# Ten even/odd sums accumulated in one PSUM bank, and three even halves moved ahead to around the logits

## The chip, the cores and the metric

The kernel runs on one core of a Trainium2 chip. The metric is device time in microseconds (us). Most executions of one kernel on one chip agree within about half a per cent; on the third chip of this study they spread over 1.5. A run is slow when it is over 1.5% above the fastest run of the same kernel. The engines are TensorE (PE in the profile; PEld is its weight load), VectorE (DVE), ScalarE (ACT), GpSimd (POOL) and SyncE (SP).

## The reference

A two-dimensional Fourier transform of each of eight batches, of which the real part is kept, feeds a mixture of experts whose assignment is greedy and global: the largest of all logits first, one expert per token, 2,496 tokens per expert.

```python
X = np.fft.fft(np.fft.fft(x, axis=1), axis=2).real      # x: 8 x 2496 x 256
x = X.reshape(19968, 256)
logits = x @ w_gate                                     # 8 experts
for idx in np.argsort(-logits.flatten()):               # greedy assignment, 2496 tokens an expert
    tok, e = idx // 8, idx % 8
    if assigned[tok] >= 0 or counts[e] >= cap: continue
    assigned[tok] = e; counts[e] += 1
for e in range(8):
    out[assigned == e] = np.maximum(x[assigned == e] @ w1[e], 0) @ w2[e]
```

## The kernel before

It has three stages. In the first (to about 98 us), x is loaded and transformed along its rows, and small matrices for the logits are prepared; the logits end this stage. In the second, **VectorE works out the assignment** (a chain of dependent steps: maxima, lists, a threshold search, ranks) while TensorE does the transform along the columns beside it. In the third, from 169 us to the end, the experts run, and TensorE is busy almost without a hole (341.04 of 356.60 us in the profile).

The column transform is made of 20 calls, `transform(n)`. Each has an even half and an odd half of ten matmuls, each into a PSUM bank of its own. With even half E and odd half O, the rows that are wanted are E + O and E - O.

```python
def transform(n):
    st = stg.tile([P, NB, 4, D], BF, tag="stage", bufs=4)
    ps = []
    def combine():                                       # run later, by flush()
        nc.vector.tensor_tensor(st[:, :, 0, :], ev, ps[1], op=AL.add)
        nc.vector.tensor_tensor(st[:, :, 3, :], ev, ps[1], op=AL.subtract)
        for q in range(2):                               # mirrored columns, sign turned
            nc.scalar.activation(st[:, :, 1 + q, P + 1:D], st[:, :, 3 * q, P + 1:D], ACT.Copy, scale=-1.0)
        # ... copies on GpSimd, store to DRAM ...
        return 1.3                                       # us of VectorE, for the pace
    for r in range(2):                                   # even half, odd half
        fps = ... psm.tile(tag="to"[n % 2], bufs=1) if r else big_ps("fftps")   # big_ps: tag "h", 3 banks
        # ... ten matmuls into fps ...
        ps.append(fps)
        if r == 0:
            ev = stg.tile([P, NB, D], FT, tag="ev", bufs=2)
            nc.scalar.copy(ev, fps)
        cost = flush()                                   # combine the transform before
        if r == 1:
            pending.append(combine)
        yield cost
```

How much of this is put beside the chain is decided when the program is built, by a model of two clocks: the chain's steps advance VectorE's clock by an estimate, and halves (and, at set places, turns of expert weights) are issued while TensorE's clock is behind it.

```python
def unit():                                              # one half, sometimes a weight turn as well
    cost = next(units, None)                             # ... False is returned when none is left
    clock["PE"] += 1.15; clock["D"] += cost; clock["n"] += 1
    if clock["n"] in TURNS: next(pieces); clock["PE"] += 0.45
for c in first_chain():
    # c: VectorE cost of a step; ... at SYNC, where VectorE waits for TensorE, the clocks are levelled
    clock["D"] += c
    while clock["PE"] < clock["D"] - 1.0 and unit(): pass
```

What is not placed there follows behind the chain, ahead of the experts. I call that the **leftover**.

## Time and profile before

| | before |
|---|---|
| time, median of the first 3 runs | 528.65 us (527.63 to 530.01) |
| span of the profiled execution | 526.0 us |
| last gate sums of the load stage start | 83.40 us |
| first matmul that turns the lists (lt) | 117.31 us |
| threshold's matmul (lev_ps), ranks (rps) | 130.71, 133.61 us |
| first expert matmul (hps) | 169.40 us |
| halves and weight turns placed before the ranks | 21 and 7 |

The rows from the last gate sums to the first expert matmul are milestones in TensorE's timeline; the last row counts instructions in the built program. From the first expert matmul to the end are 526.0 - 169.40 = 356.6 us. TensorE is busy for 341.04 us of them, and the work there is untouched by the change, so a milestone that reaches the experts late is taken to reach the end late. The lines of lt and lev_ps are shown in the prediction, those of the gate sums and the experts here (start, duration, engine and line, operation, tiles):

```profile
83.40 1.92 PE L296 MATMUL yps<-zt,g_sb 128*32 128x512 f32 x12
...
169.40 1.15 PE L1258 MATMUL hps<-xs,zball 128*128 128x384 bf16 x6
```

### The profile page before, as it was taken

What the parts mean: (1) busy time and instruction counts of PE and PEld (TensorE: products, weight loads), DVE (VectorE), ACT (ScalarE), POOL (GpSimd) and SP (SyncE); (2) the same over time, 40 slices, a digit from 0 to 9 for tenths busy, and PEclk for the clock granted to TensorE, in tenths of its full rate; (3) what the DMA queues carried; (4) which work ended last, traced back from release to release, by engine and by line L of the source; (5) the groups of instructions that cost most, each with busy time, mean ns of one, the idle gap of its engine ahead of it and who ended that gap; (6) DMA issues with size and microseconds to landing.
All of it is one profiled execution on the core that took longest, in us unless ns stands there. A gap on an engine that the chain in (4) does not pass through costs nothing. (4 is left out here: it accounts for less than half of the span.)

```text
span 526.0 us, 11245 instructions
## 1 busy us (share of the span) xinstructions
PE 463.3 (88%) x4039; PEld 351.1 (67%) x4039; DVE 374.1 (71%) x963; ACT 335.1 (64%) x760; POOL 316.0 (60%) x362
## 2 busy tenths in 40 slices
PE   0667678787799999999999999999999999999991
PEld 0544436675577665767767787777777777777771
DVE  8789997588876989779879777656644555555540
ACT  7879984156377877777867757556545455555540
POOL 7888825253132565535544446777777777777775
PEclk9968999999999999999999999999999999999997
DMA  8999938168479898422232323332222222222222
GB/s 260 319 282 306 315 118 137 26 237 280 115 234 274 203 223 169 129 92 100 99 99 92 109 79 105 124 126 87 79 84 83 77 86 90 76 71 74 73 82 61
DMA packets 35168, 74.62 MB, mean 142 GB/s; under 512 B 6112, under 2 KB 14346, under 8 KB 35104
## 3 DMA queue, kind: packets, MB, share of 16 engines
q0 software_dynamic: 23296, 42.10, 30.7%
q1 hardware_dynamic: 11808, 31.73, 17.8%
q8 instruction: 33, 0.54, 0.4%
q14 instruction: 31, 0.25, 0.2%
HBM read 51.26 MB, written 32.24 MB: 159 GB/s over the span
## 5 line engine op out<-in xcount | busy, mean ns | idle before, releaser
L1011 ACT ACTIVATE hb<-hps 128x384 bf16<-128x384 f32 (+1 forms) x319 | 142.9, 492 | 53.8 <-PE hps L1258 49.1
L1281 PE MATMUL ops<-w2t,hb 128*128 128x256 bf16 (+1 forms) x1344 | 173.6, 273 | 0.0
L1281 PEld LDWEIGHTS <-hb 128*128 128x128 bf16 (+1 forms) x1344 | 132.3, 99 | 31.6
L1285 POOL DMA_INDIRECT out_dram<-zball,rid x85 | 91.1, 1072 | 77.5 <-ACT zball L1011 59.8
L1258 PE MATMUL hps<-xs,zball 128*128 128x384 bf16 x640 | 127.5, 326 | 0.3 <-ACT hb L1011 0.2
L1258 PEld LDWEIGHTS <-zball 128*128 128x128 bf16 x896 | 84.6, 98 | 45.4 <-issue 7.4
L1015 DVE TENSOR_SCALAR hb<-hps 128x384 bf16<-128x384 f32 (+1 forms) x129 | 70.2, 549 | 45.1 <-PE hps L1258 35.3
L130 POOL DMA_INDIRECT xb<-in_x_dram,mir_i x40 | 54.6, 1364 | 11.9 <-issue 10.5
L1011 ACT ACTIVATE zball<-ops 128x256 f32<-128x256 f32 x82 | 31.5, 384 | 32.1 <-PE ops L1281 31.2
L1258 PE MATMUL hps<-xt,zball 128*128 128x384 bf16 (+1 forms) x256 | 47.7, 319 | 0.0
L286 PE MATMUL tp<-identf,xa 128*128 128x128 f32 x160 | 26.6, 330 | 17.8 <-ACT hi_cE L259 7.5
L286 PEld LDWEIGHTS tp<-identf,xa 128*128 128x128 f32 x160 | 22.8, 172 | 25.4 <-ACT zt L288 7.9
L1042 POOL COPY stage<-stage 128x258 bf16<-128x258 bf16 x40 | 17.6, 444 | 32.0 <-DVE stage L1037 28.5
L1011 ACT ACTIVATE xs<-sps 128x384 bf16<-128x384 f32 x68 | 30.2, 490 | 9.6 <-PE sps L1120 9.5
L1097 DVE TENSOR_SCALAR pt<-rampw,spot 128x193 bf16<-128x193 bf16 (+1 forms) x160 | 30.8, 285 | 0.1
L1120 PE MATMUL sps<-pt,xl 128*128 128x192 bf16 (+1 forms) x320 | 29.4, 232 | 0.1
L1120 PEld LDWEIGHTS <-xl 128*128 128x128 bf16 x320 | 25.6, 98 | 3.6 <-issue 1.4
L1234 POOL DMA_INDIRECT xg<-t_dram,ids_l x24 | 23.1, 963 | 7.3 <-issue 7.0
L1285 POOL DMA_INDIRECT out_dram<-zball,rows_l x23 | 22.3, 970 | 7.0 <-issue 2.7
L1017 DVE COPY zball<-ops 128x256 f32<-128x256 f32 (+1 forms) x26 | 11.0, 424 | 20.4 <-PE ops L1281 17.9
L1060 ACT COPY ev<-fftps 128x512 f32<-128x512 f32 x20 | 11.7, 584 | 21.2 <-PE fftps L1054 12.1
L1285 POOL DMA_INDIRECT out_dram<-wa,rid x20 | 19.8, 989 | 6.1 <-issue 2.7
(358 smaller groups left out, 780.2 us busy)
## 6 DMA issues: line engine op xcount, KB each, us to landing
t_dram<-stage SPq DMA_DIRECT2D x20, 512.0 KB
xl<-t_dram SPq DMA_DIRECT2D x20, 512.0 KB
xa<-in_x_dram SPq DMA_DIRECT2D x8, 1024.0 KB
w1raw<-in_moe_w_dram POOLq DMA_DIRECT2D x8, 512.0 KB, 8.6
w2t<-in_moe_w_dram POOLq DMA_DIRECT2D x8, 512.0 KB, 9.1
xa<-in_x_dram SPq DMA_DIRECT2D x8, 224.0 KB
out_dram<-zball,rid POOLq DMA_INDIRECT x85, 2.5
xb<-in_x_dram,mir_i POOLq DMA_INDIRECT x40, 7.8
```

What stands on the lines that cost most here:

```text
L130: nc.gpsimd.indirect_dma_start(out=bv[0:n, i, :], out_offset=None, in_=x_pairs, in_offset=bass.IndirectOffsetOnAxis(ap=mir_i[0:n, b * NK + ...
L286: nc.tensor.transpose(tp[:, blk, u, :], pv[:, 4 * c + u, blk * P:(blk + 1) * P], identf)
L1011: nc.scalar.activation(dst, src, ACT.Relu if relu else ACT.Copy)
L1015: nc.vector.tensor_scalar(dst, in0=src, scalar1=0.0, scalar2=None, op0=AL.max)
L1042: nc.gpsimd.tensor_copy(st[:, :, 1 + q, 0:P + 1], st[:, :, 3 * q, 0:P + 1])
L1060: nc.scalar.copy(ev, fps)
L1097: nc.vector.tensor_scalar(marks[n][:, f, 0:w], in0=rampw[:, 0:w], scalar1=spot[:, c:c + 1], scalar2=None, op0=AL.is_equal)
L1120: nc.tensor.matmul(into[:, :, SW - SC[cc]:], lhsT=xl[:, 2 * g + cc, j2 * P:(j2 + 1) * P], rhs=pt[:, 2 * g + cc, 0:E * SC[cc]].rearrange("p ...
L1234: nc.gpsimd.indirect_dma_start(out=xg[0:nr, q, :], out_offset=None, in_=t_dram, in_offset=bass.IndirectOffsetOnAxis(ap=d["ids"](q, nr), ax ...
L1258: nc.tensor.matmul(hps[:, 0:n], lhsT=w1t[d["e"]][:, j2, fc * P:(fc + 1) * P], rhs=d["x"](j2), start=(j2 == 0), stop=(j2 == 1))
L1281: nc.tensor.matmul(ops[0:nr, 0:D], lhsT=d["hid"][:, fc, b0:b0 + nr], rhs=w2t[d["e"]][:, fc, :], start=(fc == 0), stop=(fc == F // P - 1))
L1285: put = nc.gpsimd.indirect_dma_start(out=out, out_offset=bass.IndirectOffsetOnAxis(ap=d["rows"](b0 // P)[0:nr], axis=0), in_=ot[0:nr, :], ...
```

## The change

The intent was to relieve VectorE, the fullest engine beside the chain (busy for 31.54 of the 36.42 us from 99.05 to 135.47 us), in two ways. First, in ten of the transforms the odd half is accumulated onto the even half in the same bank, so the bank holds E + O: ScalarE copies that sum out, and VectorE needs only the one difference 2E - (E + O). Second, three even halves run before VectorE's chain begins, one after the gate sums, one after the tables are placed, one after the logits. For that the three "h" banks are taken from a pool that leaves early.

```diff
+SUMS = 10
+DONE = 3
...
     low_y()
     gate_x(B - 1, zts.pop(B - 1))
+    even_ahead(0)
     place_y(B - 1)()
+    even_ahead(1)
...                                   # behind the logits' matmuls
+        even_ahead(2)
...
+    def even_half(n):
+        # ... bank of even_ahead, or a new one of the three; ten matmuls if n >= DONE ...
+        evs[n] = stg.tile([P, NB, D], FT, tag="ev", bufs=3, name="ev")
+        if n < SUMS:
+            nc.scalar.activation(evs[n], fps, ACT.Copy, bias=0.0, scale=2.0)
+        else:
+            nc.scalar.copy(evs[n], fps)
+    def odd_half(n):
+        # ... n < SUMS: ten matmuls that accumulate into the even half's bank ...
         def combine():
-            nc.vector.tensor_tensor(st[:, :, 0, :], ev, ps[1], op=AL.add)
-            nc.vector.tensor_tensor(st[:, :, 3, :], ev, ps[1], op=AL.subtract)
+            if n < SUMS:
+                nc.scalar.copy(st[:, :, 0, :], fps)
+            else:
+                nc.vector.tensor_tensor(st[:, :, 0, :], ev, fps, op=AL.add)
+            nc.vector.tensor_tensor(st[:, :, 3, :], ev, fps, op=AL.subtract)
...
-            return 1.3
+            return 0.7 if n < SUMS else 1.3
+    def halves():
+        for n in range(SUMS + 1):
+            if n < SUMS:
+                even_half(n)
+                if n >= DONE:
+                    yield flush()
+            if n > 0:
+                cost = flush()
+                pending.append(odd_half(n - 1))
+                yield cost
+        # ... then as before ...
-    clock = {"PE": 0.0, "D": 0.0, "n": 0}
+    clock = {"PE": 0.0, "D": 0.0, "n": DONE}
```

While the "h" banks hold sums, weight turns and sorts use the odd halves' banks instead. One of two sort buffers goes.

More of the change, by code (lines that the diff above doesn't have):

```diff
@@ L101 @@
     psl = ps_cm.__enter__()
+    pst_cm = tc.tile_pool(name="psturn", bufs=1, side="right", space=PS)
+    pst = pst_cm.__enter__()
     ab = {}
@@ L281, in turn_x @@
     def turn_x(b, pv, c):
-        tp = psl.tile([P, 2, 4, P], FT, tag="tp", bufs=2, name="tp")
+        tp = pst.tile([P, 2, 4, P], FT, tag="tp", bufs=2, name="tp")
         nn = 4 if c < 2 else 2
@@ L373 @@
             xa_cm.__exit__(None, None, None)
+            pst_cm.__exit__(None, None, None)
         if b > 0:
@@ L385, with half_products, even_ahead @@
             tab_phases()
+    psm = ctx.enter_context(tc.tile_pool(name="psmid", bufs=1, side="right", space=PS))
+    NB = 2
+    begun = {}
+    def half_products(fps, n, r, acc):
+        b0, ks = NB * (n // NK), slice(n % NK * P, (n % NK + 1) * P)
+        for d0, d1, tab in ((0, P + 1, hi["c" + "EO"[r]]), (P + 1, D, hi["s" + "EO"[r]])):
+            for i in range(NK):
+                nv = rows_of(i, r)
+                first = i == 0 and (not acc or (r == 0 and d0 == 0))
+                nc.tensor.matmul(fps[:, :, d0:d1], lhsT=tab[:nv, i, ks],
+                                 rhs=zball[:nv, b0:b0 + NB, 2 * i + r, d0:d1],
+                                 start=first, stop=(i == NK - 1 and (not acc or d0 > 0)),
+                                 skip_group_check=acc)
+    def even_ahead(n):
+        fps = psm.tile([P, 512], FT, tag="h", bufs=3, name="fftps").rearrange("p (b d) -> p b d", b=NB)
+        half_products(fps, n, 0, True)
+        begun[n] = fps
     low_y()
     gate_x(B - 1, zts.pop(B - 1))
+    even_ahead(0)
     place_y(B - 1)()
+    even_ahead(1)
     iota160 = const.tile([P, E * CB], BF, name="iota160")
@@ L482, with mid @@
     moe = ctx.enter_context(tc.tile_pool(name="moe", bufs=1, side="left"))
-    psm = ctx.enter_context(tc.tile_pool(name="psmid", bufs=1, space=PS))
+    pso = ctx.enter_context(tc.tile_pool(name="pso", bufs=1, space=PS))
+    def mid(tag):
+        return pso if tag == "o" else psm
     psr_cm = [tc.tile_pool(name="psasg", bufs=1, space=PS)]
@@ L496, in spread_ps @@
             return deep["ps"].tile(shape, dt, tag=tag + "x", bufs=1, name=nm)
-        return psm.tile(shape, dt, tag=tag, bufs=n, name=nm)
+        return mid(tag).tile(shape, dt, tag=tag, bufs=n, name=nm)
     def big_ps(nm):
@@ L843, in first_strips @@
         flush()
-        bps = psm.tile([P, 512], FT, tag="o", bufs=1, name="lev_ps")
+        bps = mid("o").tile([P, 512], FT, tag="o", bufs=1, name="lev_ps")
         nc.tensor.transpose(bps[:, 0:P], lev.to_broadcast([P, P]), identf)
@@ L856, in first_strips @@
         for e0, ne, tag in ((0, 3, "t"), (3, 3, "o"), (6, 2, "t")):
-            rps = psm.tile([P, 512], FT, tag=tag, bufs=1, name="rps")[:, 0:ne * GC]
+            rps = mid(tag).tile([P, 512], FT, tag=tag, bufs=1, name="rps")[:, 0:ne * GC]
             rv, ov = (v_.rearrange("p (f k) -> p f k", k=NK) for v_ in
@@ L1020 @@
     td_v = t_dram.rearrange("(n p f) d -> n p f d", p=P, f=8)
-    NB = 2
     def flush():
@@ L1027, in flush @@
         return cost
-    def transform(n):
-        b0, kc = NB * (n // NK), n % NK
-        ks = slice(kc * P, (kc + 1) * P)
+    evs = {}
+    def even_half(n):
+        begun[n] = begun.get(n) or big_ps("fftps").rearrange("p (b d) -> p b d", b=NB)
+        fps = begun[n]
+        if n >= DONE:
+            half_products(fps, n, 0, n < SUMS)
+        evs[n] = stg.tile([P, NB, D], FT, tag="ev", bufs=3, name="ev")
[4 more added lines that the diff above has]
+    def odd_half(n):
+        fps, ev = begun.pop(n), evs.pop(n)
+        if n >= SUMS:
+            fps = mid("to"[n % 2]).tile([P, 512], FT, tag="to"[n % 2], bufs=1, name="fftps").rearrange(
+                "p (b d) -> p b d", b=NB)
+        half_products(fps, n, 1, n < SUMS)
         st = stg.tile([P, NB, 4, D], BF, tag="stage", bufs=4, name="stage")
-        ps = []
         def combine():
-            nc.vector.tensor_tensor(st[:, :, 0, :], ev, ps[1], op=AL.add)
-            nc.vector.tensor_tensor(st[:, :, 3, :], ev, ps[1], op=AL.subtract)
+            if n < SUMS:
[3 more added lines that the diff above has]
+            nc.vector.tensor_tensor(st[:, :, 3, :], ev, fps, op=AL.subtract)
             for q in range(2):
@@ L1045, in combine, with side_ps @@
                 reload(n)
-            return 1.3
-        for r in range(2):
-            fps = (psm.tile([P, 512], FT, tag="to"[n % 2], bufs=1, name="fftps") if r else big_ps("fftps")).rearrange(
-                "p (b d) -> p b d", b=NB)
-            for d0, d1, tab in ((0, P + 1, hi["c" + "EO"[r]]), (P + 1, D, hi["s" + "EO"[r]])):
-                for i in range(NK):
-                    nv = rows_of(i, r)
-                    nc.tensor.matmul(fps[:, :, d0:d1], lhsT=tab[:nv, i, ks],
-                                     rhs=zball[:nv, b0:b0 + NB, 2 * i + r, d0:d1],
-                                     start=(i == 0), stop=(i == NK - 1))
-            ps.append(fps)
-            if r == 0:
-                ev = stg.tile([P, NB, D], FT, tag="ev", bufs=2, name="ev")
-                nc.scalar.copy(ev, fps)
-            cost = flush()
-            if r == 1:
-                pending.append(combine)
-            yield cost
+            return 0.7 if n < SUMS else 1.3
+        return combine
+    def halves():
+        for n in range(SUMS + 1):
+            if n < SUMS:
+                even_half(n)
+                if n >= DONE:
+                    yield flush()
[3 more added lines that the diff above has]
+                yield cost
+        flush()
+        side["on"] = False
+        for n in range(SUMS, 4 * NT):
+            even_half(n)
+            yield flush()
+            pending.append(odd_half(n))
+            yield 0.0
+    side = {"on": True, "n": 0}
+    def side_ps(nm):
+        if not side["on"]:
+            return big_ps(nm)
+        side["n"] = 1 - side["n"]
+        return mid("to"[side["n"]]).tile([P, 512], FT, tag="to"[side["n"]], bufs=1, name=nm)
     def turn_w(e, eng=None):
@@ L1074, in turn_pieces @@
             for fh in range(2):
-                wps = big_ps("wps")
+                wps = side_ps("wps")
                 fs = slice(fh * 512, (fh + 1) * 512)
@@ L1099, in sort_mark @@
         busy["D"] += 1.1
-    a8 = [moe.tile([P, 4, 320], BF, name="a8_%d" % i) for i in range(2)]
-    for i in range(2):
-        nc.gpsimd.memset(a8[i], 0.0)
+    a8 = moe.tile([P, 4, 320], BF, name="a8")
+    nc.gpsimd.memset(a8, 0.0)
     def reload(n):
@@ L1115, in sort_call @@
         for g in gs:
-            sps = big_ps("sps")
+            sps = side_ps("sps")
             for cc in range(2):
@@ L1125, in sort_rows @@
     def sort_rows(t, part):
-        a_t = a8[t % 2]
+        a_t = a8
         if part == 1:
@@ L1159 @@
     pieces = (None for e in range(4) for _ in turn_pieces(e, "A"))
-    units = (cost for n in range(4 * NT) for cost in transform(n))
-    clock = {"PE": 0.0, "D": 0.0, "n": 0}
+    units = halves()
+    clock = {"PE": 0.0, "D": 0.0, "n": DONE}
     def unit():
```

## The prediction

> **What bounds the kernel now.** I read the page first, then the windows of the middle stage, then TensorE's waits, then the timelines of the three engines there.
>
> ```profile
> span 526.0 us, 11245 instructions
> PE 463.3 (88%) x4039; PEld 351.1 (67%) x4039; DVE 374.1 (71%) x963; ACT 335.1 (64%) x760; POOL 316.0 (60%) x362
> ...
> PE   0667678787799999999999999999999999999991
> ```
>
> Slices are 13.15 us. From slice 12 (158 us) TensorE shows a 9 to the end, and the window from 300 to 400 us has it busy for 100.00 us: the expert stage is TensorE's, so a start of that stage that moves by x moves the end by about x. Before it TensorE has gaps. The change acts between 85 and 170 us, so I cut that stretch where the assignment chain on VectorE lets go.
>
> ```profile
> core 0: us, PE busy (x) PEld busy (x) DVE busy (x) ACT busy (x) POOL busy (x), PEclk, DMA share, GB/s
> 99.05:135.47 36.42, 30.23 (x254) 24.18 (x255) 31.54 (x73) 17.47 (x38) 15.15 (x37) 1.00 0.60 203
> 135.47:169.40 33.93, 31.13 (x306) 25.40 (x304) 26.36 (x83) 22.41 (x53) 9.45 (x22) 1.00 0.72 205
> ```
>
> In the first window VectorE is the fullest (31.54 of 36.42 us), in the second TensorE (31.13 of 33.93). So the first is a chain on VectorE with transform halves put beside it, the second the transform work that was left over. The waits of TensorE from 99 to 175 us, and where they fall:
>
> ```profile
> PE fftps L1054 <- DVE stage L1038: 3.1, 3, 1.6
> PE lev_ps L845 <- DVE stage L1038: 3.1, 1, 3.1
> PE fftps L1054 <- DVE pool L470: 1.1, 1, 1.1
> PE rps L860 <- DVE ohb L850: 1.1, 1, 1.1
> ```
> ```profile
> 85.88 0.65 PE L306 MATMUL ytp<-identf,yt 96*128 96x96 f32 x4 [0.57 <-ACT yt L299]
> 87.27 0.19 PE L457 MATMUL lps_cE<-yhl,hi_cE 128*128 128x64 bf16 x1 [0.74 <-DVE yhl L310]
> ...
> 99.09 0.72 PE L1054 MATMUL fftps<-zball,hi_cE 128*128 128x258 bf16 x5 [1.14 <-DVE pool L470]
> ...
> 106.36 0.73 PE L1054 MATMUL fftps<-zball,hi_cO 128*128 128x258 bf16 x5 [1.56 <-DVE stage L1038]
> ...
> 117.31 1.04 PE L632 MATMUL lt<-identf,lists_x 128*128 128x128 f32 x8
> ...
> 130.71 0.29 PE L845 MATMUL lev_ps<-identf,s_lev 128*128 128x128 f32 x1 [3.07 <-DVE stage L1038]
> ```
> ```profile
> 101.40 0.59 ACT L1060 COPY ev<-fftps 128x512 f32<-128x512 f32 x1 [9.10 <-DVE lg L474]
> ...
> 105.75 0.41 ACT L1040 ACTIVATE stage<-stage 128x254 bf16<-128x254 bf16 x1 [2.54 <-DVE stage L1037]
> ```
> ```profile
> 103.62 1.49 DVE L599 TENSOR_TENSOR dd<-lg,mx 128x1280 bf16<-128x1280 f32 x1
> 105.03 0.68 DVE L1037 TENSOR_TENSOR stage<-ev,fftps 128x512 bf16<-128x512 f32 x1
> 105.63 0.68 DVE L1038 TENSOR_TENSOR stage<-ev,fftps 128x512 bf16<-128x512 f32 x1
> ```
>
> The reader is to see four things. TensorE's holes before the logits are 0.57 and 0.74 us. ScalarE cannot copy the first even half until 101.40, because the copy's buffer lies where the logits' scratch was (released by the last lg). VectorE's first combination stands behind dd, at 105.03. All of TensorE's waits from 99 to 170 us sum to 9.9 us.
>
> [...] In the kernel before no bank has two readers: ScalarE reads the even bank, VectorE the odd one. In the changed one ScalarE (twice) and VectorE read one bank, and the built program shows the guard: each difference on VectorE waits for ScalarE's copy of the same sum. No run yet shows its price. [...] on ScalarE each even copy starts after the negations queued before it. [...] here ten matmuls of a half take 1.11 us start to start (99.09, 99.64, 100.19)[...].
>
> **The change part by part.** Call the halves of transform n e(n) and o(n).
>
> Saved: ten of 40 VectorE combinations go. Each occupies 0.60 us start to start (105.03 to 105.63), so 6.0 us of VectorE; eight of the differences that stay lie ahead of the strips, where there were 11 pairs, so 14 x 0.60 = 8.4 us go from the chain's own engine. Three halves, 3 x 1.11 = 3.3 us, leave TensorE's stretch after 99 us.
>
> Added: e(0) and e(1) before the logits are 2.2 us into holes of 0.57 and 0.74. e(0) begins at 85.25, ends 86.36, so the transposes move from 85.88 to 86.36; e(1) follows 0.53 us later and ends at 88.00, where the logits began at 87.27: **0.73 us late**. e(2) after the logits takes the place of the 1.14 us wait. Ten copies of 0.59 us come to ScalarE.
>
> Moved, and this decides it. o(n) now accumulates into the bank that e(n) filled, so it waits for the even copy of n. That copy is still bound to the last lg, 101.29 + 0.73: copy 102.13 to 102.72, o(0) at 102.77. e(2) ended at 99.65, so TensorE stands 3.1 us. At 105 us it has done five halves, as before. Then a ring closes. There are three banks, so e(n+3) waits for difference n. ScalarE's order in the built program is even copy n+3, sum copy n+1, negations. Difference n+1 waits for sum copy n+1. From one difference to the next: difference 0.68, semaphore 0.05, e(n+3) until ScalarE starts 1.36 (99.09 to a start 0.09 us after the modeled end), even copy 0.49, sum copy 0.59, 0.04: **3.2 us a transform**, where TensorE needs 2.22.
>
> Walking that: difference 0 stands behind dd at 105.76, differences 1 to 4 come at 108.97, 112.18, 115.39 and 118.60. The chain's lists end behind difference 4, so lt comes at 119.66 instead of 117.31. From there fewer combinations win the time back: search 1 ends 3.4 us late, then TensorE is no longer ahead with two halves and a weight turn, and lev_ps comes at about 130.45 against 130.71. So the chain ends where it did, strips' marks at 141.1.
>
> But by then TensorE has done less. In the order of the two programs 21 halves and seven weight turns stand before the strips' sums (rps) in the kernel before, 18 halves (with the three ahead) and four turns in the changed one. What is left is more by 3 x 1.11 + 3 x 0.43 = **4.6 us**, in the window where TensorE is the bound. Its first half after rps no longer waits (0.58 us saved). Differences 8 and 9 stand behind the marks at 141.1, and with the banks held by them a weight turn waits about 2.2 us and the next steps 1.1 us: 3.3 us against 1.34 at the same place before, 2.0 us more. Sum: 4.6 - 0.6 + 2.0 - 0.1 (chain) = about **5.8 us later** at the experts. By idle time: 9.9 grows to about 18, +8.2, less 3.3 moved, plus 0.7 of delay: 5.6. The two agree.
>
> **Rivals.** First, the ring does not bind (the guard is cheap, the copies prompt). Then lt comes 1.4 us earlier, the strips 5.6 us earlier, and with TensorE's gaps mostly closed the experts start 2 to 5 us sooner: 524 to 527. For it: VectorE is 87% full in the first window and loses 8.4 us. Against: the order and waits of the built program are fixed. Second, hidden anyway: the halves ahead only trade a wait at 99 for one at 102, and the rest evens out: 528 to 530. For it: five halves done at 105 us both ways. Third, worse than walked: ScalarE, with ten more copies, stays behind into the second window and every even copy lags; ScalarE is only 22 of 34 us busy there, so against; 537 to 541. A transfer as the bound I exclude: reloads come tens of us before use, DMA share is 0.6 to 0.7.
>
> **Range and chances.** 528.65 + 5.6 is **534.2 us**. My walk sums some thirty handovers each good to 0.05 to 0.1 us, and the second window's stall to perhaps 2 us, so 529.5 to 538.5 holds it 8 times in 10, the low side leaving room for the second rival. Two per cent are 10.6 us: faster than 518.1 needs twice all that could be won, 0.01; slower than 539.2 needs the third rival, 0.05; within, 0.94.
>
> **What will show it.** Logits start near 88.0. o(0) waits about 3 us for the even copy. VectorE stands about 2.6 us between differences 0 and 1, waiting for ScalarE's sum copy, and differences are 3.2 us apart until lt at about 119.7. TensorE waits for differences at e(4), e(5), e(6), about 1.0 us each. lev_ps near 130.5. The first expert matmul near 175 instead of 169.40. I am wrong if VectorE takes difference 1 at once, if lt comes before 117.3, or if the experts begin before 170; and if they begin at 175 but the end does not move, the expert stage was not TensorE's alone.

The forecast: its sum stays at about 5.8 us (4.6 - 0.6 + 2.0 - 0.1, which as printed make 5.9). The durations in it are those of the profile of before: a half takes 1.11 us start to start (99.09 to 100.19), a weight turn 0.43 (119.30 to 119.73), an even copy 0.49 (119.55 to 120.04), and the 0.05 us called semaphore lie between the end of the 0.68 us at 105.63 and the odd half at 106.36. The 0.59 us of the sum copy and the 0.04 us after it are estimates; the even copy's 0.59 us and the step from the end of the 0.68 us at 105.03 to the negation at 105.75 agree with them. The order on ScalarE reads there, for one, as negations at 105.75 and 106.34, even copy at 106.67. That each difference waits for ScalarE's copy of the sum was read from the built program, and what this costs was not measured then; the profile of after has 8.3 us in six waits. Of the reloads, three are issued from 111.38 to 116.66 us and the first matmul that reads one starts at 149.75; none of the waits of TensorE listed from 99 to 175 us ends with a transfer.

## The result, and the profile after

The changed kernel took 536.41 us (median of 4 runs, 536.15 to 536.95), the kernel before 528.28 us beside it (median of 4). The ratio is **1.015**, interval 1.0123 to 1.0177. Here and below a ratio is the mean time of one kernel's fast runs over that of the other's of the same rounds, so it is not quite the ratio of the medians. The result is correct in all runs told of here.

The page of the changed kernel, in the same rows as before, with the granted clock's row (tenths of full speed; the kernel before has its own in the second fence):

```profile
span 534.3 us, 11214 instructions
PE 468.1 (88%) x4028; PEld 352.5 (66%) x4039; DVE 367.2 (69%) x953; ACT 340.2 (64%) x770; POOL 313.9 (59%) x361
...
PEclk9978889999799999999999999999999999999996
```
```profile
PEclk9968999999999999999999999999999999999997
```

VectorE has ten instructions and 6.9 us less, ScalarE ten more and 5.1 us more: the trade that was intended took place. In the fifth, sixth and eleventh slices the changed kernel's clock shows 8, 8 and 7 where the kernel before has 9; the eleventh is 134 to 147 us, in the stretch that the change acts on, the other two are in the load stage.

TensorE's timeline after, for the places that the prediction walked (start, duration, engine and line, operation, tiles, count, and in brackets the wait before it):

```profile
85.35 1.92 PE L300 MATMUL yps<-zt,g_sb 128*32 128x512 f32 x12
...
104.50 0.72 PE L401 MATMUL fftps<-zball,hi_cO 128*128 128x258 bf16 x5 [2.95 <-ACT ev L1068]
108.22 0.72 PE L401 MATMUL fftps<-zball,hi_cE 128*128 128x258 bf16 x5 [1.33 <-DVE stage L1085]
111.37 0.72 PE L401 MATMUL fftps<-zball,hi_cE 128*128 128x258 bf16 x5 [0.77 <-DVE stage L1085]
...
121.17 1.09 PE L662 MATMUL lt<-identf,lists_x 128*128 128x128 f32 x8 [0.55 <-DVE lists_x L654]
...
132.00 0.29 PE L875 MATMUL lev_ps<-identf,s_lev 128*128 128x128 f32 x1 [1.36 <-DVE s_lev L870]
...
137.50 1.29 PE L401 MATMUL fftps<-zball,hi_cO 128*128 128x258 bf16 x5
...
177.17 1.15 PE L1312 MATMUL hps<-xs,zball 128*128 128x384 bf16 x6
```

VectorE's differences in the same stretch, and what VectorE waited for from 95 to 145 us (total, times, longest):

```profile
107.48 0.68 DVE L1085 TENSOR_TENSOR stage<-ev,fftps 128x512 bf16<-128x512 f32 x1
...
110.63 0.69 DVE L1085 TENSOR_TENSOR stage<-ev,fftps 128x512 bf16<-128x512 f32 x1 [2.47 <-ACT stage L1082]
...
113.78 0.69 DVE L1085 TENSOR_TENSOR stage<-ev,fftps 128x512 bf16<-128x512 f32 x1 [1.06 <-ACT stage L1082]
```
```profile
DVE stage L1085 <- ACT stage L1082: 8.3, 6, 2.5
```

And ScalarE between the first two differences:

```profile
109.52 0.60 ACT L1068 ACTIVATE ev<-fftps 128x512 f32<-128x512 f32 x1 [0.91 <-PE fftps L401]
110.02 0.58 ACT L1082 CAST stage<-fftps 128x512 bf16<-128x512 f32 x1
```

The ring of the prediction can be read off these lines step by step. Difference 0 starts at 107.48 and frees a bank; TensorE takes the next even half (e(3)) at 108.22, after 1.33 us of standing; ScalarE copies it at 109.52, having itself waited 0.91 us for TensorE; only then, at 110.02, does it copy the sum of transform 1, whose matmuls end by 106.9 us but which stands behind the even copy in its queue; and VectorE, which has stood for 2.47 us, starts difference 1 at 110.63. From there to 113.78 are 3.15 us, and the next two differences follow at the same distance. In the kernel before VectorE has no wait of this kind: from 95 to 145 us none of its waits listed ends with ScalarE.

The milestones need one correction before they are compared. The last gate sums start at 83.40 us in the profile of before, at 85.35 in that of after. Over all profiles, whose load stages run the same instructions, this start lies anywhere from 83.39 to 86.75 us. It goes with the clock of that stage: the six profiles with 6.8 to 17.1 us at half clock before 84 us have it at 83.4 to 84.0 us, the eight with 20.5 or 23.9 us at 84.1 to 86.8 us (before 17.1 us, after 20.5 us). So the lateness of 1.95 us belongs to the execution as far as this record shows, and I give milestones **from the start of the last gate sums**:

| from the last gate sums, us | before | after | after, second profile |
|---|---|---|---|
| lt | 33.91 | 35.82 | 36.03 |
| lev_ps | 47.31 | 46.65 | 46.86 |
| rps | 50.21 | 49.61 | 50.75 |
| first expert matmul | 86.00 | 91.82 | 93.25 |
| halves, turns before rps | 21, 7 | 18, 4 | 18, 4 |

The end of the chain stays where it was and the experts are 5.8 and 7.3 us late. From the first expert matmul to the end are 534.3 - 177.17 = 357.1 us, against 356.6. So the loss is made before the experts, and it passes to the end whole.

The windows that the prediction showed of the kernel before, in the profile of after (columns as there):

```profile
99.05:135.47 36.42, 24.77 (x238) 19.30 (x236) 24.48 (x62) 18.36 (x38) 12.48 (x32) 0.97 0.43 160
135.47:175.00 39.53, 37.10 (x300) 29.00 (x304) 27.56 (x83) 25.24 (x59) 10.22 (x23) 0.94 0.72 212
```

VectorE is no longer the full engine beside the chain (24.48 of 36.42 us, was 31.54): it was relieved. But TensorE too did less there (24.77, was 30.23), and made it up in the second window, where it is the bound. The clock is 0.97 and 0.94 in these windows, 1.00 and 1.00 in the kernel before. This was not in the prediction. Its place is clear in a short window, 135 to 141 us, first of before, then of after:

```profile
135.00:141.00 6.00, 5.41 (x45) 4.29 (x44) 5.71 (x23) 1.18 (x2) 0.72 (x1) 1.00 0.22 34
```
```profile
135.00:141.00 6.00, 5.92 (x26) 3.88 (x28) 4.35 (x12) 0.45 (x1) 0.25 (x1) 0.57 0.55 92
```

TensorE is busy for longer (5.92 us against 5.41) with 26 instructions instead of 45: it runs at a granted clock of 0.57. Five matmuls that take 0.72 us elsewhere take 1.29 us there (the line at 137.50 above). The stretch at half clock itself is 133.4 to 140.2 us. Just ahead of it, from 128.7 to 132.1 us, TensorE had stood but for two lone matmuls of 0.16 and 0.29 us (the second is the lev_ps line above), waiting for VectorE's search each time.

So there were two theories to test, and a third that could make either unimportant. **Ring**: the order on ScalarE, even copy before sum copy, is what costs. **Clock**: stop-and-go on TensorE costs, by way of half-clock stretches. **Leftover**: too little TensorE work is placed beside the chain, because the pace now counts 0.7 us a combination.

### The profile page after: what moved, and what is told of

Read it like the earlier page. It is cut to its first block, busy times and chain, and to the rows that moved or that the text cites. A ratio compares the mean times of both kernels' runs of the same rounds, so it can differ in the third digit from the quotient of the medians.

```text
span 534.3 us, 11214 instructions
## 1 busy us (share of the span) xinstructions
PE 468.1 (88%) x4028; PEld 352.5 (66%) x4039; DVE 367.2 (69%) x953; ACT 340.2 (64%) x770; POOL 313.9 (59%) x361
## 5 line engine op out<-in xcount | busy, mean ns | idle before, releaser
L134 POOL DMA_INDIRECT xb<-in_x_dram,mir_i x40 | 54.0, 1349 | 11.9 <-issue 10.2
L349 DVE TENSOR_TENSOR xa<-xa,xb 128x2550 f32<-128x2550 f32 (+2 forms) x10 | 22.8, 2282 | 0.0
```

The lines of the kernel that those rows point to most:

```text
L134: nc.gpsimd.indirect_dma_start(out=bv[0:n, i, :], out_offset=None, in_=x_pairs, in_offset=bass.IndirectOffsetOnAxis(ap=mir_i[0:n, b * NK + ...
L349: nc.vector.tensor_tensor(a_t[:, i0:i1, :, 1:D], a_t[:, i0:i1, :, 1:D], b_t[:, i0:i1, ::-1, D - 1:0:-1], op=AL.add)
```

## The experiments

Twelve runs in three groups; each group shares its runs of the kernel before. The first group's kernel before took 528.96 us, the second's 528.58 us (7 runs each, on two chips). The third group fell on a chip on which the kernel before took 589.27 us; it is told of on its own.

### First group: the ring

**The changed kernel again**, without an edit.

> The changed kernel once more, unedited, for a second profile and as the base of this call. All theories: 536 to 537 us. What it tells apart: in the first profile the logits stage began 1.95 us later than before (first gate sums for the last batch at 85.35 instead of 83.40), and the granted clock was 0.57 from 135 to 141 us. If both are chance of one execution they are gone or smaller here at the same time (534 would be the time without them); if they belong to the kernel they recur.

Measured: 537.32 us, ratio 1.0166 (1.013 to 1.0201). The difference is real and repeats, and so does the ring (3.15 us a difference). This profile has half-clock stretches at 104.0 to 107.4, 131.3 to 134.7 and 144.9 to 148.3 us, of which the first profile had only one like the second, twice as long. The first of them follows the wait of 2.94 us for the even copy. So the half clock recurs, at other places, and the late load stage is smaller (84.14 us).

**Sum copy ahead of the even copy.** `flush()` runs the combination that is pending; moved ahead of the even half, it puts the sum copy and the negations before the next even copy in ScalarE's queue. Nothing else changes, and the counts of halves and turns stay 18 and 4.

```diff
+                cost = flush() if n >= DONE else 0.0
                 even_half(n)
                 if n >= DONE:
-                    yield flush()
+                    yield cost
```

> The sum copy and the negations of an earlier transform are put on ScalarE ahead of the even copy of a later one; TensorE's and VectorE's order stays. Theory A (the ring of difference, even half, even copy, sum copy, difference paces the chain at 3.15 us a transform): the ring has no even half in it any more, VectorE's wait between the first two differences falls from 2.5 to about 1.1 us, lt comes 2 to 3 us earlier, and the time falls to 532 to 534. Theory B (too little TensorE work was put beside the chain, so what is left over decides; the ring is slack): lt earlier or not, the time stays at 535.5 to 536.5.

Measured: 531.18 us, ratio **1.0038** (1.0005 to 1.0071). The first five differences now follow at 1.6 to 2.5 us, and VectorE's wait for sum copies falls from 8.3 to 3.8 us, shown in the second fence over the same 95 to 145 us:

```profile
107.56 0.68 DVE L1085 TENSOR_TENSOR stage<-ev,fftps 128x512 bf16<-128x512 f32 x1
109.19 0.69 DVE L1085 TENSOR_TENSOR stage<-ev,fftps 128x512 bf16<-128x512 f32 x1 [0.95 <-ACT stage L1082]
...
111.71 0.69 DVE L1085 TENSOR_TENSOR stage<-ev,fftps 128x512 bf16<-128x512 f32 x1 [0.44 <-ACT stage L1082]
```
```profile
DVE stage L1085 <- ACT stage L1082: 3.8, 5, 1.4
```

From the last gate sums, lt comes at 32.96, lev_ps at 42.26, the experts at 87.73. The ring was there, and moving two lines recovers about 6 of the 8 us. But one thing does not fit if the ring is all: the chain now reaches lev_ps 5.1 us sooner than in the kernel before, and yet the experts start 1.7 us later. Between lev_ps and the experts 45.47 us pass, against 38.69 in the kernel before: 6.8 us more, with the same 18 halves and 4 turns placed before the ranks as in the changed kernel. That speaks for the leftover as a second part.

**Difference ahead of the sum copy.** Here VectorE's read of the bank is put first, and ScalarE's copy behind it.

```diff
         def combine():
-            if n < SUMS:
-                nc.scalar.copy(st[:, :, 0, :], fps)
-            else:
+            if n >= SUMS:
                 nc.vector.tensor_tensor(st[:, :, 0, :], ev, fps, op=AL.add)
             nc.vector.tensor_tensor(st[:, :, 3, :], ev, fps, op=AL.subtract)
+            if n < SUMS:
+                nc.scalar.copy(st[:, :, 0, :], fps)
```

> In the combination the difference on VectorE goes ahead of the sum copy on ScalarE, so ScalarE waits for VectorE in the shared bank and not the reverse; same instructions. Theory A: VectorE no longer waits for ScalarE's sum copies (8.3 us of waits fall below 2), differences follow TensorE at about 2.2 us, lt comes about 3 us earlier, the strips 4 us earlier, 531 to 534. Theory B: the chain ends earlier, but TensorE's leftover does not shrink and ScalarE's later copies hold banks: 535 to 537.

Measured: 532.54 us (531.34 to 536.54), ratio 1.0061 (1.0031 to 1.009). VectorE has no wait for a sum copy left, and differences 0 and 1 run back to back. What comes instead is on TensorE: it waits for ScalarE's copies, now the last to read a bank, 2.8 us once and 1.1 us once, and in the profiled execution, which was the slowest of the five, its clock is half from 106.6 to 113.5 us, and the third difference stands 2.98 us for TensorE. So lt comes at 37.56 us from the last gate sums, later than in the changed kernel: the "3 us earlier" missed in this execution, while the times held.

**Sum copied by VectorE.** One word is changed, `nc.scalar.copy` to `nc.vector.tensor_copy`. The bank then has one reader, and VectorE gets its ten instructions back.

> The sum copy goes to VectorE as well, so no two engines share a bank's readers apart from the even copy; VectorE gets back the ten operations that the change took from it. Theory A: no wait of VectorE on ScalarE's sum copies, lt near the kernel before plus 0.7 to 1.5 us, 531 to 535. Theory B (VectorE's saved work is what counts, and its loss hurts): slower than the changed kernel, above 537.

Measured: 533.42 us (531.17 to 535.28), ratio 1.0075 (1.0027 to 1.0122). Here too differences 0 and 1 follow at once, and here too the third comes late, in a half-clock stretch (105.5 to 112.3 us). lt comes at 34.78, 0.9 us later than in the kernel before, as expected.

What follows from the four: each of three different ways to open the ring wins 4 to 6 us of the medians against 537.32. Which way matters less than that it is open. None reaches the kernel before.

### Second group: the clock, and the two parts of the change alone

**Waits filled.** Matmuls whose results nobody reads are put where TensorE stands: the third even half is computed three times and the eleventh twice, and 15 wide matmuls go into the banks of the second search's sum, of lev_ps and of rps. The outcome is the same numbers.

```diff
+        for _ in range(2):
+            half_products(begun[2], 2, 0, True)
...
+    def fill(ps, k):
+        for _ in range(k):
+            nc.tensor.matmul(ps, lhsT=onesb, rhs=..., start=True, stop=True)
...
+        fill(bps, 5)                       # lev_ps; 7 in the search, 3 in rps
...
+            for _ in range(1+1 if n == SUMS else 1):
                 half_products(fps, n, 0, n < SUMS)
```

> The changed kernel with idle matmuls (results never used, or the same half computed again) in TensorE's waits before o(0), the second search sum, lev, rps and after e(10): 15 of 512 columns and three halves again, sized to end before the wait does. Theory C (beside the ring, the stop-and-go of TensorE lets its granted clock fall to 0.50 for 3.4 us or multiples of it between 100 and 150 us, which none of it did in the kernel before): the dips at 104 to 112, 130 to 140 and 144 to 148 us are gone or fewer, the time falls from 537 by 1.5 to 3 us to 534 to 535.5 although TensorE has 6.5 us more to do. Rival (the dips fall into time that TensorE waits anyway): the time stays at 536 to 538.

Measured: 534.35 us (533.92 to 535.62), ratio 1.0113 (1.0081 to 1.0144). From 84 us to the experts its profile has no stretch under full clock, the ring is unchanged (3.15 us), and the window around the dip in the changed kernel reads as follows, first of the changed kernel, then of the filled one:

```profile
132.00:141.00 9.00, 8.12 (x39) 5.11 (x41) 7.15 (x17) 2.06 (x4) 1.20 (x2) 0.62 0.51 118
```
```profile
132.00:141.00 9.00, 7.95 (x58) 5.59 (x57) 7.73 (x23) 2.57 (x5) 1.24 (x2) 1.00 0.55 117
```

So useless work made the kernel 2.1 to 3.0 us faster (against 536.41 and 537.32). The intervals of the ratios overlap at their ends, and the 537.32 us are from another chip, so the size is rough; the clock column is not. Nor does all of it lie in the stretch that was filled: from the gate sums, the experts start at 91.51 us, only 0.3 and 1.7 us sooner than in the two profiles of the changed kernel.

**Waits filled in the kernel with the sum copy ahead.** The same fillers, in slightly other numbers, on top of copy_first.

> The version with the sum copies ahead of the later even copies (531.2), with idle matmuls in the same waits (15 of 512 columns and four halves again). Theory C: no dips of the clock from 100 to 150, and with the ring and the dips both gone the three halves that were moved show at last: 526.5 to 529. Rival: 530.5 to 532.

Measured: 529.96 us, ratio 1.0026 (0.9989 to 1.0064), between the two expectations; no clock dip from 84 us to the experts, which start 86.83 us from the last gate sums. Against copy_first that is 1.2 us by the medians, inside the intervals, so whether the filling won anything here is not shown. This is the fastest of the changed kernels on the two fast chips, and not told apart from the kernel before.

**Halves ahead only.** SUMS is 0, so all twenty transforms have two banks and two VectorE operations, and the three even halves still go ahead.

```diff
-SUMS = 10
+SUMS = 0
...
-            yield flush()
+            if n >= DONE:
+                yield flush()
```

> Only the three even halves ahead; each transform keeps two banks and two operations on VectorE (no sums). Theory A (ring from the sums in one bank is the main cost): no ring, no wait of o(0) for the even copy; TensorE has 3.3 us less to do after the logits, which start 0.73 us later, while all three big banks are taken at 99 us: 526 to 529.5. Rival (the halves ahead are themselves the loss, through the later logits and the banks they hold): 531 to 534.

Measured: 536.43 us, ratio 1.0146 (1.0117 to 1.0174). **Both expectations missed.** The profile tells of two things. The three banks stay held until combination 0, which stands behind VectorE's own steps, so TensorE waits 6.6 us in one piece at 109 us. And the pace, which counts three halves as done and a full 1.3 us a combination, puts 18 halves and 4 turns ahead of lt, where the changed kernel has 13 and none: lt comes at 46.51 us from the last gate sums, not 35.82. So this run does not measure one part alone. It shows only that the halves ahead did not pay in this form.

**Sums only.** DONE is 0 and the three `even_ahead` calls are gone.

> Only the sums in one bank for the first ten transforms; no half ahead of or right behind the logits. Theory A: the ring is there as in the changed kernel (differences 3.15 us apart, VectorE waits 7 to 9 us for sum copies), and 3.3 us of TensorE work return to the stretch after 99 us: 536 to 540. Rival (the sums are harmless or good without the halves ahead): 526 to 531.

Measured: 533.12 us, ratio 1.0088 (1.0053 to 1.0123), between the two expectations. The ring is there (gaps of 0.77 us on TensorE again), a clock dip between 84 us and the experts is not, and lt and lev_ps come sooner than in the kernel before (30.44 and 42.18 against 33.91 and 47.31), because the pace places only 9 halves ahead of lt. The experts come at 89.70, 3.7 us late: only 16 halves and 2 turns stand before the ranks. Again a chain that is early and experts that are late.

### Third group: the pace, on a slower chip

On this chip the kernel before took 589.27 us (583.3 to 592.31, 11 runs, two of them slow; 588.81 without these). In the four profiles taken here the extra 60 us are in the expert stage. From 300 to 400 us TensorE is busy for 100.00 us in copy_first on the fast chip, and for 87.82 us in copy_first_mid here; what makes the holes was not looked into. From the first expert matmul to the end the four profiles have 417.5, 414.6, 416.1 and 417.3 us. That stage alone scatters by 3 us, which is what the experiments are about, so the times decide little, and **I read the milestones instead, which lie before the experts**. There is one profile of each, and none of the kernel before on this chip.

**Sum copy ahead, and a pace of 1.0 us**, in place of 0.7: more work beside the chain.

```diff
-            return 0.7 if n < SUMS else 1.3
+            return 1.0 if n < SUMS else 1.3
```

> copy_first with one number changed: the pace counts 1.0 us instead of 0.7 us of VectorE for a combination whose sum ScalarE copies, so that more TensorE work is put beside the chain. In the built order 20 halves and 6 weight turns stand before the strips' sums, where copy_first has 18 and 4 and the kernel before 21 and 7. Theory L (the leftover is what keeps copy_first from beating the kernel before): 2 halves and 2 turns, 3.1 us, move from the stretch in which TensorE is the bound into gaps beside the chain, of which TensorE had about 5 us in copy_first, so the experts begin 1 to 3 us sooner and the time is 528 to 530.3. Rival (the work merely delays the chain by as much as it takes off later): 530.5 to 532, lev_ps about 3 us later than in copy_first.

Measured: 588.08 us (587.32 without one run of the slow state), ratio 0.9999 (0.9931 to 1.0066). TensorE's first expert matmul, first of copy_first (its last gate sums start at 85.16), then of this kernel (85.54):

```profile
172.89 1.15 PE L1313 MATMUL hps<-xs,zball 128*128 128x384 bf16 x6
```
```profile
169.48 1.15 PE L1313 MATMUL hps<-xs,zball 128*128 128x384 bf16 x6
```

The experts start at 83.94 us from the last gate sums: 3.8 us sooner than in copy_first and 2.1 us sooner than in the kernel before. lev_ps is 2.8 us later than in copy_first, as the rival had it, and the experts come sooner all the same. The clock is a rival for a part of the 3.8 us: this profile has 3.4 us at half clock between 84 us and the experts, that of copy_first 6.8 us.

**Sum copy ahead, and the old pace of 1.3 us.** The edit is `return 1.3`.

> As copy_first_mid, with the old 1.3 us: 24 halves and 8 turns before the strips' sums. Theory L: TensorE has no gap left beside the chain but the chain's own matmuls now stand behind more work, so the gain stops: 528 to 531, lev_ps 3 to 5 us later than copy_first. Rival (the leftover is the whole rest of the cost, so more is better): 526 to 528. Second rival (the chain becomes the bound): over 532.

Measured: 588.93 us, ratio 1.0039 (0.997 to 1.0109). The experts start at 85.38, so 2.4 us sooner than in copy_first but 1.4 later than with 1.0. lev_ps is 8.2 us later than in copy_first, more than the 3 to 5 expected. Of the three paces tried, 1.0 us has the earliest experts, as the leftover theory had it; here the profile has 6.8 us at half clock again.

**Sums only, sum copy ahead.** The edit of copy_first on sums_only.

> sums_only with the even copy behind the sum copy on ScalarE: no halves ahead, ten sums in one bank, no ring. Pace as in sums_only, so 16 halves and 2 turns before the strips' sums. Theory A (the ring is the main cost wherever sums are shared): differences under 2.7 us apart, lt 1 to 2 us sooner than sums_only's 114.0, and the time 1.5 to 4 us under sums_only: 529.5 to 531.5. Rival L (in sums_only the leftover is the cost, not the ring, since TensorE is the bound behind the strips and the chain has slack): no VectorE wait on sum copies, lt and lev_ps sooner, but the experts begin no sooner: 532 to 534.

Measured: 594.48 us, ratio 1.0141 (1.0075 to 1.0208), which the verdict calls unclear and which is not better than the 1.0088 of sums_only on the other chip. By milestones lt comes 1.6 us sooner than in sums_only (28.82) and the experts 2.4 us sooner (87.29), as theory A had it; the first differences are 2.1, 2.1 and 3.2 us apart, so "under 2.7" holds for most of them. Neither of the two profiles has a half-clock stretch between 84 us and the experts, so the clock is no rival here. The time does not show this, and I leave it open.

**Even copies with a place of their own.** The buffers of the even copies move to a pool that does not lie on the logits' scratch, so the first three need not wait for the last lg.

```diff
+    evp = ctx.enter_context(tc.tile_pool(name="evp", bufs=1, side="left"))
...
-        evs[n] = stg.tile([P, NB, D], FT, tag="ev", bufs=3, name="ev")
+        evs[n] = evp.tile([P, NB, D], FT, tag="ev", bufs=3, name="ev")
```

> The changed kernel with the buffers of the even copies in a place of their own, so that the first three need not wait for the last lg. My walk put 3.1 us of TensorE's standing at the first odd half down to this wait, but holds the first difference to stand behind dd all the same, with all banks taken until it runs: the wait moves from the first odd half to the fourth even half, lt stays within 0.7 us of the changed kernel's 120.2, and the time is 535.5 to 537.5. Rival (the wait at the first odd half is itself a part of the loss): lt 2 us sooner, 533 to 535.

Measured: 598.51 us, ratio 1.0205 (1.0143 to 1.0266). The wait at the first odd half is gone, and the fourth even half waits 4.5 us for the first difference in its place, the longest of five here:

```profile
PE fftps L401 <- DVE stage L1086: 6.8, 5, 4.5
```

From the second on, differences stay 3.15 us apart, and lt comes at 36.96, about 1 us later than in the two profiles of the changed kernel (the expectation allowed 0.7), not 2 us sooner. The first difference starts where it did, 22.2 us from the last gate sums against 22.1, and the second comes 4.2 us behind it, in a half-clock stretch (107.8 to 111.2 us). The rival falls: the wait of 2.95 us that stands out first in TensorE's list was only a place where TensorE stood, not a cause.

The milestones together, all from the last gate sums in us:

| kernel | lt | lev_ps | experts | halves, turns before rps | us at half clock, 84 us to the experts |
|---|---|---|---|---|---|
| before | 33.91 | 47.31 | 86.00 | 21, 7 | none |
| after | 35.82 | 46.65 | 91.82 | 18, 4 | 6.8 |
| copy_first | 32.96 | 42.26 | 87.73 | 18, 4 | 6.8 |
| copy_first_mid | 35.35 | 45.09 | 83.94 | 20, 6 | 3.4 |
| copy_first_full | 38.80 | 50.43 | 85.38 | 24, 8 | 6.8 |
| sums_only | 30.44 | 42.18 | 89.70 | 16, 2 | none |

## Why the prediction was right or wrong

It said 534.2 us and within 2 per cent; the time was 536.41 us, inside its range, 1.5 per cent slower. By its own steps:

- **Logits late by 0.73 us**: from the last gate sums the first logits matmul is 4.62 us (89.97 us in the profile) against 3.87, 0.75 later. Held.
- **First odd half waits 3.1 us for the even copy**: 2.95 and 2.94 us in two profiles. Held as a wait. copies_early shows that it is not a loss of its own, which the walk implied, since it had difference 0 behind dd either way.
- **Ring of 3.2 us**: 3.15 us, and the stall before difference 1 was 2.47 us against 2.6. Held, down to the order of the queue. copy_first opens it and wins about 6 us. In milestones the ring had eaten the 4.4 us by which lev_ps then comes sooner (42.26 against 46.65).
- **TensorE's waits at e(4) to e(6), "about 1.0 us each"**: 0.77 us each, the first at e(3) 1.33. Slightly over.
- **lt at 119.66, lev_ps at about 130.45, experts near 175**: 119.22, 130.05 and 175.22 when the profile is shifted to the load stage of the kernel before (less 1.95 us). Held.
- **Leftover of 4.6 us more, and 2.0 us of a stall, less 0.6**: 6.0 us more between lev_ps and the experts than in the kernel before. Measured 6.5 and 7.7 us in the two profiles of the changed kernel, which have half-clock stretches there, and 6.0 in the filled one, which has none (but one half more). Its parts held less well than their sum: the weight turn that was to wait about 2.2 us waited 1.04 and 2.37 us. copy_first_mid points to such work being worth about what was counted: 2 halves and 2 turns (3.1 us) put back beside the chain went with experts 3.8 us sooner. One profile each, on two chips, with 3.4 us less at half clock.
- **The sum, about 5.8 us** (the terms as printed make 5.9, and the 534.2 us takes the 5.6 of the count by idle time): the medians differ by 8.1 us, and the time is 2.2 us over the 534.2. The mechanism was right, the sum short. **What it left out is TensorE's clock**: it counted every half at 1.11 us, at full clock. Between 84 us and the experts the two profiles of the changed kernel have 6.8 and 10.2 us at half clock, that of the kernel before has none. With the waits filled, no dip and the ring untouched, the time is 534.35 us, 5.8 us over the kernel before of its chip. How much of the 2.2 us the change makes is not settled: against the filled kernel, the two profiles lose 0.3 and 1.7 us between the gate sums and the experts, and 1.6 and 0.4 us in the load stage, where the three run the same instructions.
- **Luck in one profile.** In the first one the experts are 5.8 us late from the gate sums, as walked, although 6.8 us there ran at half clock. Two errors met: the slow matmuls, and the weight turn's wait of 1.04 us where 2.2 was forecast. In the second profile that wait is 2.37 us and the experts are 7.3 us late.
- **A miscount without consequence**: ahead of the marks at 141.1 us the trace of the kernel before has ten pairs of combinations, not 11 (the eleventh starts at 141.13), so 12 x 0.60 = 7.2 us go from VectorE there, not 8.4. Only the first rival used the number.

Of its rivals, the first (no ring) falls by the 3.15 us, the second (hidden anyway) by the interval, and the third (ScalarE behind) was not needed: ScalarE has 25.24 of 39.53 us in the second window.

Of the missed term the runs show this: the granted clock in the dips is 0.50; between 84 us and the experts they last 3.4 or 6.8 us; their places differ between executions of one kernel (133.4 us in the first profile of the changed kernel, 104.0, 131.3 and 144.9 us in the second); and in the two filled kernels there are none. In the changed kernel 3.4 us with two lone matmuls of 0.16 and 0.29 us were followed, 1.3 us later, by half clock. One wait of 2.95 us was not followed by it, those of 2.94 and 3.0 us in the next profile and in vec_copy were. What brings the half clock, and how little activity is enough for it, these runs do not show. I had read waits as idle time only, and did not ask what they do to the clock, although the page of the kernel before shows a clock of 0.6 in its third slice, in the load stage.

Open: whether the change also shifts the load stage a little on the average (its end scatters by 3.4 us, and there is one profile of before), what slows the experts on the third chip, and the time of copy_first_mid on a fast chip, where its milestones suggest some 2 us under the kernel before.

## What to carry to other kernels

Where two engines read one PSUM bank, one waited for the other here (VectorE for ScalarE's copies 8.3 us in six waits, and 3.8 us in five when the copies came first in ScalarE's queue), so ask what else stands ahead in each engine's queue: an order of two copies on ScalarE was worth 6 us, nearly as much as the 6.9 us of work that the change took from VectorE. Where a pace or a scheduler places work beside a chain, a cheaper step changes how much is placed, and that must be set again (0.7 to 1.0 us here went with experts 3.8 us sooner, in one profile each). Short waits on TensorE went with 6.8 and 10.2 us at half clock here, and with none when they were filled, so before adding short waits to a stretch that is nearly full, look at the granted clock and not at the waits alone.
